# Segment means of h in two whole operations with the sums of h behind them on VectorE, and another order of products in the w3 groups

## The chip, the cores and the metric

The kernel runs on one core of a Trainium2 chip. The core has TensorE (PE, matrix products, with a queue of its own for loading weights, PEld), VectorE (DVE), ScalarE (ACT), GpSimd (POOL) and SyncE (SP, which here only issues DMAs). Each engine works through its instructions in the order of its queue and waits at semaphores for the others. Accumulators lie in eight banks of PSUM, everything else that is worked on in SBUF.

The metric is the time on the device in microseconds, the median of several runs. Before the change it is 1487.03 us (six runs, 1484.1 to 1489.75).

## The reference

A recurrent attention block A and a mixer block B, each between layer norms with conditioning:

```python
x = A_x                                    # 1 x 2048 x 1024
sa, ca, ga, sb, cb, gb = split(silu(c) @ w_mod)
h = layernorm(x) * (1 + ca) + sa
x = x + ga * A(h, mem0, Wq, Wk, Wv, Wo, seg_len=32)
h = layernorm(x) * (1 + cb) + sb
x = x + gb * B(h, w1, w2, w3, w4)

def A(x, mem0, ...):                       # 32 heads of 128, 8 memory rows
    mem = mem0
    for s in range(64):                    # 64 segments of 32 rows
        h = concat([mem, x[segment s]])    # 40 rows
        q, k, v = h @ Wq, h @ Wk, h @ Wv
        o = softmax(mask(q k^T * scale)) v @ Wo
        mem, out_s = o[:8], o[8:]

def B(x, w1, w2, w3, w4):
    h = gelu(layernorm(x) @ w1)
    hs = shifted_quarters(h) @ w2
    x1 = x + hs
    return x1 + gelu(layernorm(x1) @ w3) @ w4     # w3: 1024 x 3584
```

## The kernel before

**Start.** Sixteen row tiles of x are normalized, turned over by TensorE and written as h, transposed, into the tile `hh` (128 partitions, 8 blocks of 128 features, about 2100 columns); lines L436 (VectorE) and L438 (ScalarE) apply the conditioning on the way out of PSUM. Beside each transpose a small product (L427) adds up the 32 rows of every segment into a PSUM bank, `hsum` (named `small_ps` in the profile: 128 partitions, 8 blocks x 64 segments). While later tiles are being normalized, TensorE already runs the projections of the first heads ("wave 0", `proj_main`, L318), whose accumulators are emptied by `evac` (L122 on ScalarE, L127 on VectorE). Three accumulators go round.

**Segment means and the memory.** The memory rows that a segment hands on are first estimated from the segment means. `g_prep` (from L457) makes `hbar`, the means after conditioning, out of `hsum`, the scale `cm` and the shift `sm_`; column 0 is different, since the first segment sees `mem0` (`m0`). Before the change this is one operation per block of features, in turn on ScalarE (L462) and VectorE (L460), then L464 and L465 for column 0. `g_v` multiplies the means by chunks of Wv (L477) and copies the result out (`vbarT`, L478), `g_o` multiplies by chunks of Wo (L491) into a bank that L494 and L495 copy into the memory columns of `hh`. The chunks of 1 MB pass through six buffers `wchunk`, loaded by SP (L473, L487) whenever one is free. One remaining projection of wave 0 is put after each `g_v` or `g_o`. The order of instructions on each engine in this part of the kernel comes from a scheduler that works from the program, its dependencies and estimated times; `keep_order` binds an instruction to its place in the program, and `add_manual_dep` adds a dependency.

**Sums of h.** The main projections of the other heads multiply in two-by-two blocks with seven products instead of eight (Strassen's scheme in Winograd's form). It needs sums of blocks of `hh`: `S1`, `S2`, `S4` and, in place, A11 - A21, for two pairs of column chunks (L519 to L522), and sums `T1` to `T4` of the weights per head (L566 to L569). The products are L623, their results leave through copies (`snap`, L591) and joins (L595). Attention runs between them: scores (L717), exponential (L721, ScalarE), mask (L723, VectorE), products with V (L734, after V was transposed by a DMA, L667), the reciprocals of the sums (L736) and the scaled results `O` (L741 on VectorE, L739 on ScalarE).

**Middle.** The Wo products (L905), the second layer norm, w1 and w2 follow; `Ba` (L1172, L1173) makes x1 and its row sums, `ln_sums` normalizes it, and a DMA transposes it into `z2a` and `z2b`, the two pairs of column chunks of the last stage.

**The w3 and w4 stages** stand in the order of the program on every engine (`manual_schedule`). For each of two pairs, `w3_stage` runs seven groups of 512 columns of w3. A group is again seven products of two halves q, each half four matmuls (L1244). Four banks `bank_b`, two `bank_e` and two `bank_d` hold the results. Products with A11 and B11 start bank_b; ScalarE copies it (`snap`, L1209) as `s1`; products of S2 and T2 are added to the same bank, which is copied again (`s2`); products of S3 and T3 are added, and at last those of A22 and T4. Products of A12 and B21 go to bank_e, products of S1 and T1 to bank_d (copied as `s5`), where those of S4 and B22 are added. `join` adds a bank and a copy on VectorE (L1252), `gelu` follows on ScalarE (L1248). The sums of weights for the next group are L1098, `w3_sums`. The w4 stage (L1295) has the same form over 14 blocks. The next pair starts when the w4 stage of the first ends.

Of the kernel before, what the change touches and what calls it, by code (L numbers as in the profile page):

```python
# [9 lines left out]
BF16 = mybir.dt.bfloat16  # L10
# [9 lines left out]
P = 128  # L20
# [40 lines left out]
def kernel(ctx, tc, A_x, A_mem0, A_Wq, A_Wk, A_Wv, A_Wo, A_seg_len, B_x, B_w1, B_w2, B_w3, B_w4, c, w_mod, out,  # L61
# [105 lines left out]
    def first_pass(late_hook):  # L167
# [288 lines left out]
        def g_prep():  # L456
            gs["hbar"] = sb1.tile([P, KT, NSEG], BF16, name="hbar")  # L457
            for kt in range(KT):
                if kt % 2:
                    nc.vector.tensor_scalar(gs["hbar"][:, kt, :], hsum[:, kt, :], cm[:, kt:kt + 1], sm_[:, kt:kt + 1], ALU.mult, ALU.add)  # L460
                else:
                    nc.scalar.activation(gs["hbar"][:, kt, :], hsum[:, kt, :], ACT.Identity, bias=sm_[:, kt:kt + 1], scale=cm[:, kt:kt + 1])  # L462
            first = sb1.tile([P, KT], F32, name="first")
            nc.vector.tensor_tensor(first[:], hsum[:, :, 0], cm[:], ALU.mult)  # L464
            nc.vector.tensor_tensor(gs["hbar"][:, :, 0], first[:], m0[:], ALU.add)  # L465
            gs["vbarT"] = sb1.tile([P, H, NSEG], BF16, name="vbarT")
# [48 lines left out]
        for p in range(2):  # L515
            c0, c1 = slice(2 * p * CH, (2 * p + 1) * CH), slice((2 * p + 1) * CH, (2 * p + 2) * CH)
            A11, A12, A21, A22 = hh[:, 0:4, c0], hh[:, 4:8, c0], hh[:, 0:4, c1], hh[:, 4:8, c1]
            S1, S2, S4 = (hsp.tile([P, 4, CH], F16, name=f"hs{j}{p}")[:] for j in (1, 2, 4))
            keep_order(nc.vector.tensor_tensor(S1, A21, A22, ALU.add))  # L519
            keep_order(nc.vector.tensor_tensor(S2, S1, A11, ALU.subtract))  # L520
            keep_order(nc.vector.tensor_tensor(S4, A12, S2, ALU.subtract))
            keep_order(nc.vector.tensor_tensor(f16(A21), A11, A21, ALU.subtract))  # L522
            hA.append((A11, A12, S4, A22, S1, S2, f16(A21)))
# [635 lines left out]
        def Ba(t):  # L1159
            def f():  # L1160
# [13 lines left out]
                z = tp.tile([P, D], BF16, name="z")  # L1174
                ln_sums(bsm, z[:], x1b[:], sums)
                zs[t] = z
# [50 lines left out]
        def w3_stage(pair):  # L1227
# [6 lines left out]
            for g in range(7):  # L1234
# [29 lines left out]
                for q in prod("b", S2, T2, False):  # L1264
                    st[q]["s2"] = snap(st2, st[q]["b"])
                for q in range(2):
                    st[q]["d"] = psd.tile([P, 512], F32, name="bank_d")
                for q in prod("d", S1, T1, True):
                    st[q]["s5"] = snap(stA, st[q]["d"])
                for q in prod("b", S3, T3, False):  # L1270
# [815 lines left out]
```

## Time and profile before

| | us |
|---|---|
| median of six runs | 1487.03 (1484.1 to 1489.75) |
| the profiled execution, whole time | 1487.09 |
| its span, first to last instruction | 1485.3 |
| PE busy in the span | 1425.8 (96%) |
| DVE, ACT, POOL busy | 887.4, 684.9, 363.7 |
| PE waiting for hbar (L477) | 4.6, once |
| PE waiting for copies of banks in w3 (L1244) | 8.8, four times |
| one 128x512 f32 sum on DVE (L1252), one copy of a bank on ACT (L1209) | 0.69, 0.58 |
| one 128x1920 sum of h on DVE (L519) | 1.15 |

How to read it: a group line gives the source line, the engine, the operation, what it writes and reads and its shape, and in brackets how long the engine sat idle before it and what ended that idling. Matmuls are pipelined: a 512-wide one is shown as 0.379 us long while the next starts 0.216 us after it. The profile also gives the clock that was granted to TensorE, 0.993 on the mean of this execution.

### The profile page before, as it was taken

What the parts mean: (1) busy time and instruction counts of PE and PEld (TensorE: products, weight loads), DVE (VectorE), ACT (ScalarE), POOL (GpSimd) and SP (SyncE); (2) the same over time, 40 slices, a digit from 0 to 9 for tenths busy, and PEclk for the clock granted to TensorE, in tenths of its full rate; (3) what the DMA queues carried; (4) which work ended last, traced back from release to release, by engine and by line L of the source; (5) the groups of instructions that cost most, each with busy time, mean ns of one, the idle gap of its engine ahead of it and who ended that gap; (6) DMA issues with size and microseconds to landing.
All of it is one profiled execution on the core that took longest, in us unless ns stands there. A gap on an engine that the chain in (4) does not pass through costs nothing. (4 is left out here: it accounts for less than half of the span.)

```text
span 1485.3 us, 24759 instructions
## 1 busy us (share of the span) xinstructions
PE 1425.8 (96%) x9254; PEld 754.8 (51%) x9254; DVE 887.4 (60%) x1946; ACT 684.9 (46%) x1443; POOL 363.7 (24%) x526
## 2 busy tenths in 40 slices
PE   5898999999999999999998999999997999999998
PEld 3565556565555555555554444444443444444443
DVE  5218777777676777667653345344245658666684
ACT  2715666665666665655551021123466661046400
POOL 8402100000000000000001223213023654545525
PEclk9999999999999999999999999999999999999999
DMA  9587967867777777778579999994398774477812
GB/s 321 191 285 157 189 155 184 200 146 173 165 171 177 190 157 179 158 167 183 112 171 315 354 305 369 320 229 156 113 291 244 238 241 149 135 231 250 283 40 78
DMA packets 404149, 303.48 MB, mean 204 GB/s; under 512 B 199082, under 2 KB 356778, under 8 KB 402226
## 3 DMA queue, kind: packets, MB, share of 16 engines
q1 hardware_dynamic: 365904, 242.06, 61.0%
q10 hardware_dynamic: 29330, 30.89, 7.0%
q0 software_dynamic: 8784, 28.85, 6.4%
q8 instruction: 74, 1.21, 0.4%
q14 instruction: 57, 0.47, 0.1%
HBM read 200.56 MB, written 50.63 MB: 169 GB/s over the span
## 5 line engine op out<-in xcount | busy, mean ns | idle before, releaser
L905 PE MATMUL acc<-wstream,OTc 128*128 128x512 bf16 x960 | 209.0, 379 | 5.5 <-DMA OTc<-OTx_d 2.4
L623 PEld LDWEIGHTS <-T 128*128 128x128 f16 x1408 | 130.9, 98 | 119.5 <-issue 2.7
L591 ACT COPY snap<-acc 128x480 f32<-128x480 f32 x264 | 145.9, 563 | 91.2 <-PE acc L623 83.4
L623 PE MATMUL acc<-hh,T 128*128 128x480 bf16 (+1 forms) x704 | 163.8, 367 | 0.0
L623 PE MATMUL acc<-hs,T 128*128 128x480 f16 x704 | 158.3, 367 | 0.7 <-ACT snap L591 0.7
L905 PEld LDWEIGHTS <-OTc 128*128 128x128 bf16 x960 | 93.4, 98 | 117.7 <-issue 3.8
L1244 PEld LDWEIGHTS <-ring 128*128 128x128 f16 (+1 forms) x784 | 77.8, 99 | 107.8 <-issue 17.9
L759 POOL DMA_DIRECT2D OTx_d<-OT x32 | 24.8, 774 | 436.6 <-DMA OT<-O 390.8
L721 ACT ACTIVATE E<-ps_s 99x495 bf16<-99x495 f32 (+2 forms) x160 | 87.1, 545 | 45.9 <-PE ps_s L717 45.4
L623 PE MATMUL acc<-hh,wq 128*128 128x480 bf16 x464 | 103.9, 366 | 0.0
L741 DVE TENSOR_TENSOR O<-ps_o,rin_all 99x384 bf16<-99x384 f32 (+1 forms) x192 | 97.2, 510 | 3.7
L734 PE MATMUL ps_o<-V,E 99*128 99x129 bf16 (+1 forms) x704 | 79.7, 220 | 10.1 <-DMA V<-VT 4.6
L1295 PEld LDWEIGHTS <-hq 128*128 128x128 bf16 (+1 forms) x560 | 54.8, 98 | 66.1
L595 DVE TENSOR_TENSOR KT<-acc,snap 128x480 bf16<-128x480 f32 x116 | 74.9, 655 | 21.2 <-PE acc L623 18.8
L1209 ACT COPY snap<-bank_b 128x512 f32<-128x512 f32 x72 | 40.5, 582 | 100.9 <-PE bank_b L1295 63.2
L1098 DVE TENSOR_TENSOR ring<-ring 128x1024 f16<-128x1024 bf16 (+1 forms) x64 | 80.0, 1270 | 4.4 <-PE bank_b L1295 4.0
L734 PEld LDWEIGHTS <-E 99*128 99x128 bf16 (+1 forms) x704 | 56.3, 98 | 48.0 <-issue 7.5
L1013 ACT ACTIVATE u<-x,ln_nmr,ln_rstd 128x1024 bf16<-128x1024 f32 x16 | 19.7, 1231 | 127.8 <-DVE ln_nmr L1012 125.5
L723 DVE TENSOR_TENSOR E<-E,maskB 99x495 bf16<-99x495 bf16 (+1 forms) x128 | 48.1, 376 | 49.6 <-ACT E L721 47.6
L1295 PE MATMUL bank_b<-ring,hq 128*128 128x512 f16 (+1 forms) x336 | 73.2, 379 | 0.0
L595 DVE TENSOR_TENSOR VT<-acc,snap 128x480 bf16<-128x480 f32 x90 | 58.0, 651 | 24.9 <-PE acc L623 20.8
L1248 ACT ACTIVATE hq<-join 128x512 bf16<-128x512 f32 x84 | 52.8, 630 | 42.6 <-DVE join L1252 42.5
(243 smaller groups left out, 2521.5 us busy)
## 6 DMA issues: line engine op xcount, KB each, us to landing
wstream<-in_A_Wo_dram SPq DMA_DIRECT2D x31, 1024.0 KB, 10.9
OTx_d<-OT POOLq DMA_DIRECT2D x32, 512.0 KB, 7.2
wstream<-in_B_w_dram SPq DMA_DIRECT2D x28, 512.0 KB, 5.7
OTc<-OTx_d SPq DMA_DIRECT2D x14, 1024.0 KB, 8.4
ring<-in_B_w_dram SPq DMA_DIRECT2D x28, 512.0 KB, 6.4
ring<-in_B_w_dram SPq DMA_DIRECT2D x8, 1792.0 KB, 10.9
wq<-in_A_Wq_dram SPq DMA_DIRECT2D x16, 512.0 KB, 5.0
wk<-in_A_Wk_dram SPq DMA_DIRECT2D x16, 512.0 KB, 7.3
```

What stands on the lines that cost most here:

```text
L591: nc.scalar.copy(t[:], st[q][bank][:, 0:CH])
L595: nc.vector.tensor_tensor(view(d, i), chunks(st[q][bank]), chunks(st[q][s_]), ALU.add)
L623: nc.tensor.matmul(acc[:, 0:CH], lhsT=B[:, k, :], rhs=A[:, k, :], start=(j in (1, 2, 5) and k == 0), stop=(k == 3), skip_group_check=True)
L721: nc.scalar.activation(E[:rows, 0:o], ps[:rows, 0:o], ACT.Exp, scale=DH ** -0.5)
L723: nc.vector.tensor_tensor(E[:rows, 0:o], E[:rows, 0:o], mk[:rows, 0:o], ALU.mult)
L734: nc.tensor.matmul(ps[:, i, :], lhsT=state["e", h, t // 5][:k, c:c + P], rhs=V[:k, t, 0:DH + 1], start=True, stop=True)
L741: nc.vector.tensor_tensor(O[:rows, ts[0]:ts[0] + n, :], ps[:rows, 0:n, 0:DH], rin[:, :, None].to_broadcast([rows, n, DH]), ALU.mult)
L905: mm = nc.tensor.matmul(accs[tt][:], lhsT=ot[hl // 4][:, hl % 4, tt * P:(tt + 1) * P], rhs=woc[hl // 4][:, hl % 4, :], start=(h == 0), sto ...
L1098: return nc.vector.tensor_tensor(dst, a, b, op)
L1244: nc.tensor.matmul(acc[:], lhsT=B[:, k, q * P:(q + 1) * P], rhs=A[:, k, :], start=(start and k == 0), stop=(k == 3), skip_group_check=True)
L1248: nc.scalar.activation(hq[a][f][:, g * 2 + q, :], src[:], ACT.Gelu_apprx_tanh)
L1295: nc.tensor.matmul(acc[:], lhsT=L3[:, k, i * P:(i + 1) * P], rhs=R3[:, k, :], start=(start and k == 0), stop=(k == 13), skip_group_check=True)
```

## The change

Three edits. In `g_prep` the means of all blocks are made by two operations on VectorE over the whole tile, with scale and shift broadcast along the segments, and column 0 by a third. The eight sums of h are no longer bound to their place in the program; instead the first of each pair gets a dependency on the last operation of `g_prep`. In `w3_stage` the product of S1 and T1 (bank_d) with its copy stands before the product of S2 and T2 (bank_b) with its copy. In `Ba` an assignment to a Python dictionary moves up by a statement.

```diff
         def g_prep():
             gs["hbar"] = sb1.tile([P, KT, NSEG], BF16, name="hbar")
-            for kt in range(KT):
-                if kt % 2:
-                    nc.vector.tensor_scalar(gs["hbar"][:, kt, :], hsum[:, kt, :], cm[:, kt:kt + 1], sm_[:, kt:kt + 1], ALU.mult, ALU.add)
-                else:
-                    nc.scalar.activation(gs["hbar"][:, kt, :], hsum[:, kt, :], ACT.Identity, bias=sm_[:, kt:kt + 1], scale=cm[:, kt:kt + 1])
-            first = sb1.tile([P, KT], F32, name="first")
-            nc.vector.tensor_tensor(first[:], hsum[:, :, 0], cm[:], ALU.mult)
-            nc.vector.tensor_tensor(gs["hbar"][:, :, 0], first[:], m0[:], ALU.add)
+            hs = sb1.tile([P, KT, NSEG], F32, name="hs")
+            nc.vector.tensor_tensor(hs[:], hsum[:], cm[:, :, None].to_broadcast([P, KT, NSEG]), ALU.mult)
+            nc.vector.tensor_tensor(gs["hbar"][:], hs[:], sm_[:, :, None].to_broadcast([P, KT, NSEG]), ALU.add)
+            gs["done"] = nc.vector.tensor_tensor(gs["hbar"][:, :, 0], hs[:, :, 0], m0[:], ALU.add)
             gs["vbarT"] = sb1.tile([P, H, NSEG], BF16, name="vbarT")
...
-            keep_order(nc.vector.tensor_tensor(S1, A21, A22, ALU.add))
-            keep_order(nc.vector.tensor_tensor(S2, S1, A11, ALU.subtract))
-            keep_order(nc.vector.tensor_tensor(S4, A12, S2, ALU.subtract))
-            keep_order(nc.vector.tensor_tensor(f16(A21), A11, A21, ALU.subtract))
+            s1 = nc.vector.tensor_tensor(S1, A21, A22, ALU.add)
+            tc.add_manual_dep(s1.ins, gs["done"].ins.name, mybir.DependencyInfo(mybir.DependencyClass.Sync, mybir.DependencyReason.DATA), reason="segment means first")
+            nc.vector.tensor_tensor(S2, S1, A11, ALU.subtract)
+            nc.vector.tensor_tensor(S4, A12, S2, ALU.subtract)
+            nc.vector.tensor_tensor(f16(A21), A11, A21, ALU.subtract)
...
-                z = tp.tile([P, D], BF16, name="z")
+                zs[t] = z = tp.tile([P, D], BF16, name="z")
                 ln_sums(bsm, z[:], x1b[:], sums)
-                zs[t] = z
...
                 dve(T4, B21, T2, ALU.subtract)
-                for q in prod("b", S2, T2, False):
-                    st[q]["s2"] = snap(st2, st[q]["b"])
                 for q in range(2):
                     st[q]["d"] = psd.tile([P, 512], F32, name="bank_d")
                 for q in prod("d", S1, T1, True):
                     st[q]["s5"] = snap(stA, st[q]["d"])
+                for q in prod("b", S2, T2, False):
+                    st[q]["s2"] = snap(st2, st[q]["b"])
                 for q in prod("b", S3, T3, False):
                     join(1, 1, q, "b", "s5")
```

## The prediction

> **What bounds the kernel now.** The page first, for which engine carries the span:
>
> ```profile
> span 1485.3 us, 24759 instructions
> PE 1425.8 (96%) x9254; PEld 754.8 (51%) x9254; DVE 887.4 (60%) x1946; ACT 684.9 (46%) x1443; POOL 363.7 (24%) x526
> ```
>
> TensorE is busy for 96%, so only what moves its gaps moves the time. Next the waits of PE (total us, times, longest), where I look for gaps that the edited lines own:
>
> ```profile
> PE bank_b L1244 <- ACT snap L1209: 8.8, 4, 3.2
> PE acc L477 <- DVE hbar L465: 4.6, 1, 4.6
> PE ps_o L734 <- DVE O L741: 3.7, 1, 3.7
> ```
>
> The first is the bank copy in the w3 stage, the second the segment means, the third sits where the sums of h now run. The stages around the last two (length, busy time of each engine, clock, DMA share, GB/s):
>
> ```profile
> 60.00:75.00 15.00, 10.43 (x133) 7.38 (x131) 2.66 (x9) 8.61 (x23) 0.00 (x0) 0.89 0.04 6
> 111.00:130.00 19.00, 14.21 (x126) 9.85 (x125) 15.10 (x27) 9.55 (x28) 9.07 (x12) 0.99 0.88 189
> 130.00:150.00 20.00, 19.87 (x139) 11.41 (x138) 17.81 (x51) 12.25 (x32) 1.60 (x4) 0.92 0.62 132
> 150.00:300.00 150.00, 149.68 (x1104) 88.33 (x1101) 107.72 (x282) 95.02 (x228) 12.88 (x32) 1.00 0.80 178
> ```
>
> PE idles 4.6 us in the first and 4.8 in the second, and loses clock behind each gap (0.89, 0.92); from 150 on it is full, so what is won before stays won. PE's timeline (start, us, what):
>
> ```profile
> 65.23 1.78 PE L318 MATMUL acc<-hh,wk 128*128 128x480 bf16 x8
> 71.59 3.55 PE L477 MATMUL acc<-hbar,wchunk 128*128 128x64 bf16 x64 [4.57 <-DVE hbar L465]
> 74.95 1.84 PE L318 MATMUL acc<-hh,wq 128*128 128x480 bf16 x8
> ...
> 129.44 0.34 PE L734 MATMUL ps_o<-V,E 99*128 99x129 bf16 x3 [3.73 <-DVE O L741]
> 129.62 1.74 PE L623 MATMUL acc<-hh,T 128*128 128x480 f16 x4
> ```
>
> After 4.57 us of idling, 64 matmuls take 3.36 us to the next line; 32 of them take 0.93 further on, so 1.5 us is half clock. After 3.73 us four take 1.74 for 0.97. What ACT and DVE did meanwhile:
>
> ```profile
> 62.48 4.98 ACT L438 ACTIVATE hh<-pt,saT,ca1T 128x160 bf16<-128x160 bf16 x14
> 67.26 0.64 ACT L122 CAST VT<-acc 128x480 bf16<-128x480 f32 x1
> ```
>
> ```profile
> 127.82 0.42 DVE L566 TENSOR_TENSOR T<-wk,wq 128x512 f16<-128x512 bf16 x1 [3.90 <-DMA wk<-in_A_Wk_dram]
> ```
>
> Last, the w3 stage, PE and then ACT:
>
> ```profile
> 1132.67 1.02 PE L1244 MATMUL bank_b<-zs,ring 128*128 128x512 f16 x4 [1.66 <-ACT snap L1209]
> ...
> 1140.32 3.41 PE L1244 MATMUL bank_b<-zs,ring 128*128 128x512 f16 x8 [2.45 <-ACT snap L1209]
> ...
> 1164.29 1.89 PE L1244 MATMUL bank_d<-zs,ring 128*128 128x512 f16 x8
> ...
> 1311.02 3.40 PE L1244 MATMUL bank_b<-zs,ring 128*128 128x512 f16 x8 [3.25 <-ACT snap L1209]
> ```
>
> ```profile
> 1165.41 0.59 ACT L1209 COPY snap<-bank_d 128x512 f32<-128x512 f32 x1 [0.26 <-PE bank_d L1244]
> ...
> 1310.38 1.07 ACT L1209 COPY snap<-bank_b 128x512 f32<-128x512 f32 x2 [29.56 <-DMA xb<-x1b_d]
> ```
>
> Only the first group of each pair has gaps; twelve of fourteen are gapless.
>
> **The change part by part**
>
> *Segment means.* Removed: four ACT and four DVE operations in turn (0.40 and 0.34 us) and two small ones. The chain was slow because its ACT half stood behind L438 and three L122 evacuations: it began at 62.17 and ended at 71.46. Added, all on DVE, free at 62.40: a product out of PSUM, a sum, and the first column. A 128x512 f32 operation of two tensors takes 0.69 (L1252), the column 0.20 (L465): done near 64.0. PE ends its L318 at 66.85, so the means no longer hold it. What is late next is the accumulator: the first Wv product takes the one that ACT evacuates at 67.26 to about 67.85. PE restarts at 67.9, after 1.05 us of idling instead of 4.57: 3.7 us. Gaps of 1.66 and 1.43 us in the w3 stage are followed by full spacing (four matmuls in 1.02), those of 2.03 and more by half, so I take full clock: 1.5 us more. Together **-5.2**. Bounds: -3.7 (half clock after all) to -5.4. The weight chunks issued after each freed slot move with PE: the one freed first landed 7.3 to 8.6 us after its issue and is needed 12.7 us after.
>
> *Sums of h.* Seven of the eight 128x1920 sums (1.07 us apart) leave the stretch 111 to 122 and run behind the means. In the built order five stand ahead of the first vbarT copy, two between copies. From 64.0 five end at 69.4, the copy at 69.8; PE wants that accumulator back for the third Wv product at about 71.4, after two Wv products and an L318. Later copies have over 1 us too. Who reads vbarT comes 20 us later. Cost 0, covered by those matmuls; with the sums held until the last h is written (67.3) it would be 2.3 us of PE. The in-place sum of the first pair waits for a product that runs at 62, the other stays near 111.
>
> At 111 DVE now finishes its T sums at about 115 instead of 122.2, so the masks of E follow ACT's exponentials (118.35 on) at once, and the T sum that waits for wk (127.82, a DMA issued behind two transposes on SP) stands behind the first two O's in the queue instead of ahead of them. On old times: the first outs products wait for the transpose of V issued at 113.64, which lands 7.2 us on, 120.84 (1.45 us of PE idle, for 0.89 at 122.69 before). Walking the new PE order from there with 0.2 us per 480-wide matmul, PE meets the queue behind the T sum near 129.9 and loses about 0.5, 0.2, 0.3 and 0.5 us in short waits, and reaches the L328 products of the second group at 133.6 instead of 137.18: **-3.6**. Bounds: -1.9 (a half-clock stretch after the 1.45) to -6.1 (0.89 + 3.73 idle and 1.5 of clock all gone).
>
> *w3 order.* Old order: bank_b, bank_e, bank_b (S2,T2), bank_d (S1,T1), bank_b (S3,T3). Each bank_b product waits for ACT's copy of what it adds to. With bank_d ahead, the S2 product has more cover and the S3 product has none but the other half of S2. ACT's queue changes alike: copies of bank_d ahead of the second of bank_b.
> First group of pair 0: bank_d fills the 1.66 us gap, but the end is set by ACT, whose two gelus wait until 1138.57 for a join that waits for the last transpose of z. Then come two copies more ahead of the one PE waits for, 0.47 apart: S3 starts at 1141.28 instead of 1140.32, **+1.0** (0.9 to 1.1), half clock behind it as before.
> First group of pair 1: ACT is held until 1310.38 by the output DMAs. Before, S2 ran at 1311.02 at half clock (3.25 for 1.73), then bank_d, and S3 at 1315.98. Now bank_d runs in the gap (its T1 is ready by 1307.4), S2 at 1311.02 after 1.7 us of idling at full clock, copies at 1312.92, 1313.39 and 1313.87, S3 at 1314.5: **-1.5**. Bounds -1.5 to +0.2 (half clock).
> Gapless groups: no row shows a product on the bank just copied. Nearest is bank_d at 1164.29: its copy begins 1.12 us after the product and ends at 1165.99; PE goes on 0.055 after a copy (1310.965 to 1311.02), thus 1.76 after the start, where two products take 1.727. So 0.03 per group, **+0.4** in twelve; bounds 0 and 0.2 x 12 = 2.4 (a copy that begins late by an idle stretch of ACT, 0.26).
>
> [...] The rows: gaps of 2.45 and 3.25 us each cost a stretch of 3.3 us at half speed, 1.4 and 1.7 did not. [...] I stay with the rows.
>
> *The rest.* `zs[t]` in Ba is assigned one statement earlier: no instruction, 0. No DMA is added or removed, and the queues of SP and POOL keep their order. Behind PE's order from about 140 to the w3 stage nothing differs.
>
> **Sum.** -5.2 - 3.6 + 1.0 - 1.5 + 0.4 = -8.9 against the profiled execution: span 1485.3, 1487.09 in all, which is 0.06 above the median 1487.03. Result **1478**.
>
> **Rivals**
> - *DMA holds the second gap anyway.* If V's transpose or wk comes later than read here, PE waits in place of DVE, and only the means pay: 1487.1 - 5.2 - 0.1 = 1482. For: the 3.90 us of wk. Against: its T sum now stands behind work PE needs. 0.17.
> - *Sums ahead of the copies stall the Wv products*: +2.3, 1480.5. For: five in one queue. Against: the first four read h written before 60, and only the fifth reads the last chunk. 0.10.
> - *Slower: the S3 product waits out both copies.* If PE resumes only when the second copy is done, 1.12 + 0.86 + 0.585 + 0.055 = 2.62 for 1.73, 0.9 per group, 12.6 in fourteen, +3.3 with the other terms: 1490.5. It decides from 0.66 us per group on. For: the margin is under zero. Against: each half waits for its own copy. 0.05.
> - *The change does not do what it says*: PE would be held at 67 by the accumulator for as long as by the means. Its evacuation at 67.26 excludes more than 1.1 us of that.
>
> **Numbers.** Likeliest case 0.65, the three rivals 0.32, the rest 0.03. Its own range is 1474 (all upper gains) to 1481.5; with the first two rivals and the medians' scatter 1473.5 to 1483.5, leaving out the slow one and tails. About 0.2% (3 us) is what a measurement can tell: faster means below 1484.1, which holds the likeliest case and nearly all of the first two rivals, 0.90; same 0.05; slower 0.05.
>
> **What would show it.** L477 starting 1 us after L318 at full spacing; no 3.7 us wait on O; S3 of pair 0 about 1 us later after its gap and of pair 1 sooner; gaps of some 30 ns before S3 in the other groups. Wrong if those gaps exceed 0.2 us, if PE idles 2 us or more before the third Wv product, or if a half-clock stretch follows the short gaps.

## The result, and the profile after

The changed kernel takes 1480.25 us (median of 20 runs, 1478.37 to 1483.86) against 1486.65 us for the kernel before (46 runs): a ratio of 0.9957, 95% interval 0.9947 to 0.9967, 6.4 us faster. The profiled execution has a span of 1477.9 us, 1479.68 in all; both are 7.4 below those of before. The head of its page:

```profile
span 1477.9 us, 24760 instructions
...
PE 1422.9 (96%) x9254; PEld 752.4 (51%) x9254; DVE 884.6 (60%) x1943; ACT 684.0 (46%) x1439; POOL 360.7 (24%) x526
```

**Segment means.** TensorE's timeline of the changed kernel around them (start, us, what, and in brackets the idle time before and what ended it):

```profile
65.73 1.78 PE L318 MATMUL acc<-hh,wk 128*128 128x480 bf16 x8
68.49 2.03 PE L473 MATMUL acc<-hbar,wchunk 128*128 128x64 bf16 x64 [0.98 <-ACT VT L122]
70.35 1.78 PE L318 MATMUL acc<-hh,wq 128*128 128x480 bf16 x8
```

and VectorE's:

```profile
62.80 0.68 DVE L459 TENSOR_TENSOR hs<-small_ps,cm 128x512 f32<-128x512 f32 x1
63.52 0.69 DVE L460 TENSOR_TENSOR hbar<-hs,sm 128x512 bf16<-128x512 f32 x1
64.25 0.19 DVE L461 TENSOR_TENSOR hbar<-hs,m 128x8 bf16<-128x8 f32 x1
64.58 1.16 DVE L515 TENSOR_TENSOR hs<-hh 128x1920 f16<-128x1920 bf16 x1
...
70.05 0.42 DVE L474 CAST vbarT<-acc 128x256 bf16<-128x256 f32 x1
```

The means are done at 64.44 us (64.25 and 0.19). TensorE waits 0.98 us, for the accumulator that ScalarE empties and not for them, and its 64 matmuls take 1.86 us to the next line instead of 3.36. The first vbarT copy ends at 70.47; the third product of means and Wv, which needs that accumulator, starts at 71.97, without a wait.

**The stretch where the sums of h were.** First the stages (length, busy time of PE, PEld, DVE, ACT, POOL with instruction counts, clock, DMA share, GB/s), then the waits of 0.7 us and more that TensorE still has in the stretch, with the second group's wv products (L328):

```profile
60.00:75.00 15.00, 14.02 (x199) 9.14 (x198) 11.11 (x16) 8.30 (x21) 0.00 (x0) 1.00 0.28 90
111.00:130.00 19.00, 16.38 (x126) 9.57 (x124) 10.20 (x28) 9.80 (x24) 3.80 (x7) 1.00 0.95 207
130.00:150.00 20.00, 18.74 (x146) 11.01 (x144) 16.21 (x48) 14.12 (x36) 1.86 (x5) 1.00 0.86 176
```

```profile
116.22 0.33 PE L731 MATMUL ps_o<-V,E 104*128 104x129 bf16 x3 [1.32 <-DMA V<-VT]
...
125.97 0.34 PE L731 MATMUL ps_o<-V,E 99*128 99x129 bf16 x3 [0.72 <-DVE E L720]
...
129.08 1.53 PE L328 MATMUL acc<-hh,wv 128*128 128x199 bf16 x16 [0.16 <-DVE VT L592]
...
135.29 0.40 PE L731 MATMUL ps_o<-V,E 99*128 99x129 bf16 x4 [1.05 <-DVE E L720]
```

The same wv products before:

```profile
137.18 1.54 PE L328 MATMUL acc<-hh,wv 128*128 128x199 bf16 x16
```

The 3.73 us wait for O is gone, the wait for the transpose of V has come (1.32), and the second group's wv products start at 129.08. Counted from the wk product ahead of the means (65.73, before 65.23) that is 63.35 us instead of 71.95: 8.6 us won. The last line is new: a wait of 1.05 us. ScalarE shows why:

```profile
131.44 2.01 ACT L679 ACTIVATE wstream<-wstream 128x2048 bf16<-128x2048 bf16 x1
...
133.35 0.67 ACT L718 ACTIVATE E<-ps_s 99x495 bf16<-99x495 f32 x1
```

The exponential that this E needs stands behind a square of the weight guard (L679), which adds up the squares of a part of w3. When it is done, at 134.02, VectorE has an O and a product of a row ahead of the mask, which starts at 134.82. At a mark far behind, the product that waits for a transpose of V at 625 us, the lead is smaller. After and before:

```profile
624.99 0.33 PE L731 MATMUL ps_o<-V,E 104*128 104x129 bf16 x3 [0.90 <-DMA V<-VT]
```

```profile
631.76 0.33 PE L734 MATMUL ps_o<-V,E 104*128 104x129 bf16 x3 [0.90 <-DMA V<-VT]
```

Counted in the same way it is 7.3 us (559.26 against 566.53): 1.3 of the 8.6 were given back.

**The w3 stage.** TensorE in the first group of pair 0 and of pair 1, then what ScalarE and VectorE did in pair 0:

```profile
1117.76 1.89 PE L1240 MATMUL bank_b<-z2a,ring 128*128 128x512 bf16 x8 [1.86 <-POOL ln_ve L1149]
...
1127.18 1.50 PE L1240 MATMUL bank_b<-zs,ring 128*128 128x512 f16 x4 [1.43 <-ACT snap L1205]
1133.45 3.57 PE L1240 MATMUL bank_b<-zs,ring 128*128 128x512 f16 x8 [4.77 <-ACT snap L1205]
1136.82 2.39 PE L1240 MATMUL bank_d<-zs,ring 128*128 128x512 f16 x8
1139.05 3.62 PE L1240 MATMUL bank_b<-z2a,ring 128*128 128x512 bf16 x16
...
1304.93 1.89 PE L1240 MATMUL bank_b<-zs,ring 128*128 128x512 f16 x8 [1.52 <-ACT snap L1205]
1308.36 1.89 PE L1240 MATMUL bank_b<-zs,ring 128*128 128x512 f16 x8 [1.55 <-ACT snap L1205]
```

```profile
1130.72 1.23 ACT L1244 ACTIVATE hq<-join 128x512 bf16<-128x512 f32 x2 [3.59 <-DVE join L1248]
1131.86 1.05 ACT L1205 COPY snap<-bank_d 128x512 f32<-128x512 f32 x2
1132.80 1.08 ACT L1205 COPY snap<-bank_b 128x512 f32<-128x512 f32 x2
```

```profile
1130.00 1.29 DVE L1248 TENSOR_TENSOR join<-bank_e,snap 128x512 f32<-128x512 f32 x2 [11.99 <-DMA z2b<-z]
```

The first and the seventh product of pair 0 before:

```profile
1125.71 2.95 PE L1244 MATMUL bank_b<-z2a,ring 128*128 128x512 bf16 x8 [2.03 <-POOL ln_ve L1152]
...
1145.30 3.62 PE L1244 MATMUL bank_b<-z2a,ring 128*128 128x512 bf16 x16
```

In pair 0 the product with S3 waits 4.77 us and then runs at half clock (eight matmuls in 3.57 us, elsewhere in 1.89; the granted clock is 0.50 from 1133.5 to 1136.5). What it waits for is a chain: its copy stands behind the copies of bank_d, these behind the gelus, these behind joins, and the first join waits for the last transposes of z. From the first product of the group to the seventh (A22 by T4, the first eight of the sixteen at 1139.05) it takes 21.29 us; before 19.59. S3 starts 15.69 us after the first product, before 14.61. In pair 1 there are two short waits at full clock (eight matmuls in 1.89 behind each), 13.75 us to the seventh product; before it was 15.28, with one wait of 3.25 us and half clock behind it (eight in 3.40, granted clock 0.50). The other twelve groups repeat every 12.11 us, before 12.08.

### The profile page after: what moved, and what is told of

It reads as the page before. It is cut to its first block, busy times and chain, and to the rows that moved or that the text cites. A ratio compares the mean times of both kernels' runs of the same rounds, so it can differ in the third digit from the quotient of the medians.

```text
span 1477.9 us, 24760 instructions
## 1 busy us (share of the span) xinstructions
PE 1422.9 (96%) x9254; PEld 752.4 (51%) x9254; DVE 884.6 (60%) x1943; ACT 684.0 (46%) x1439; POOL 360.7 (24%) x526
## 5 line engine op out<-in xcount | busy, mean ns | idle before, releaser
L620 PEld LDWEIGHTS <-T 128*128 128x128 f16 x1408 | 130.6, 97 | 119.5 <-issue 2.0
L620 PE MATMUL acc<-hh,T 128*128 128x480 bf16 (+1 forms) x704 | 163.1, 366 | 0.3 <-DVE VT L592 0.3
L620 PE MATMUL acc<-hs,T 128*128 128x480 f16 x704 | 157.1, 366 | 0.7 <-ACT snap L588 0.6
L620 PE MATMUL acc<-hh,wq 128*128 128x480 bf16 x464 | 103.9, 366 | 0.0
L592 DVE TENSOR_TENSOR VT<-acc,snap 128x480 bf16<-128x480 f32 x90 | 58.1, 652 | 24.8 <-PE acc L620 20.4
```

The costliest lines, as they stand in the source:

```text
L592: nc.vector.tensor_tensor(view(d, i), chunks(st[q][bank]), chunks(st[q][s_]), ALU.add)
L620: nc.tensor.matmul(acc[:, 0:CH], lhsT=B[:, k, :], rhs=A[:, k, :], start=(j in (1, 2, 5) and k == 0), stop=(k == 3), skip_group_check=True)
```

## The experiments

All were run beside the kernel before, whose medians were 1485.5 to 1487.3 us. Executions reach the wk product ahead of the means 64.97 to 66.38 us after their start, so positions in this table are counted from that product, in us; below it is called the reference product. "To w3" is where the first w3 product starts, "w3 on" the time from there to the end of the span, the next two the first group of each pair from its first to its seventh product.

| kernel | 2nd group's wv products | to w3 | w3 on | pair 0 | pair 1 | median (runs) | ratio to before (95%) |
|---|---|---|---|---|---|---|---|
| before | 71.95 | 1060.48 | 359.59 | 19.59 | 15.28 | 1486.65 (46) | |
| after | 63.35 | 1052.03 | 360.14 | 21.29 | 13.75 | 1480.25 (20) | 0.9957 (0.9947, 0.9967) |
| a_means | 66.76 | 1054.64 | 356.79 | 18.12 | 13.77 | 1480.22 (8) | 0.9962 (0.9948, 0.9976) |
| b_front | 63.27 | 1051.85 | 357.07 | 18.29 | 13.77 | 1477.59 (12) | 0.9949 (0.9933, 0.9965) |
| c_w3 | 72.12 | 1059.50 | 359.71 | 20.84 | 13.75 | 1487.93 (12) | 1.0007 (0.9996, 1.0018) |
| d_p1 | 63.10 | 1051.73 | 356.83 | 18.09 | 13.81 | 1476.56 (6) | 0.9939 (0.9922, 0.9956) |
| v1_gelu | 63.41 | 1053.70 | 354.23 | 16.21 | 12.27 | 1476.13 (4) | 0.9931 (0.9914, 0.9947) |
| m_pool | 62.96 | 1050.47 | 356.66 | 15.70 | 13.75 | 1475.01 (4) | 0.9921 (0.9904, 0.9937) |
| o_pool | 63.08 | 1053.19 | 356.55 | 15.46 | 13.77 | 1482.96 (10) | 0.9969 (0.9953, 0.9986) |
| g_guard | 63.08 | 1058.16 | 361.69 | 22.10 | 13.75 | 1487.95 (10) | 1.0009 (0.9999, 1.0018) |
| f_wk | 68.52 | 1056.54 | 359.23 | 20.43 | 13.75 | 1483.06 (1) | |
| v2_new0 | 63.21 | 1052.81 | 361.08 | 23.17 | 12.28 | 1481.91 (5) | 0.9961 (0.9947, 0.9975) |
| v2_guard | 63.11 | 1058.08 | 362.25 | 25.25 | 12.27 | 1487.09 (11) | 1.0001 (0.9991, 1.0011) |
| m_late1 | 63.39 | 1056.39 | 355.39 | 15.70 | 12.27 | 1475.06 (5) | 0.9928 (0.9914, 0.9943) |

"To w3" scatters: after, v1_gelu, m_pool and m_late1 issue the same instructions up to there and lie between 1050.47 and 1056.39. A single profile thus places the w3 stage only to some 6 us, while a group within it is read to a few hundredths. Its length can still differ from execution to execution: pair 0's first group, with the same w3 instructions in after, c_w3, f_wk and g_guard, takes 20.43 to 22.10 us. The scatter comes in behind the 625 us mark: there the eight kernels with the front of the changed one (after, b_front, d_p1, v1_gelu, m_pool, o_pool, v2_new0, m_late1) lie between 558.85 and 559.94, a_means at 561.42 and before at 566.53. The ratios are each taken beside their own runs of the kernel before. Medians of different kernels are not: where two are compared below, differences of 2 us, the spread of the medians of the kernel before, show nothing by themselves.

### The three parts, one by one

**a_means**: the changed kernel with the sums of h kept in place and the old order in w3 (the edit of b_front, below, besides this one).

```diff
-            s1 = nc.vector.tensor_tensor(S1, A21, A22, ALU.add)
-            tc.add_manual_dep(s1.ins, gs["done"].ins.name, ...)
+            keep_order(nc.vector.tensor_tensor(S1, A21, A22, ALU.add))
...
```

> Only the segment means are new; the sums of h stay where the kernel before has them and the w3 groups keep the old order. Theory (the parts add up): TensorE starts the first Wv product about 1 us after the last wk product instead of 4.6, at full clock, and the second wq product stands 5.1 us earlier, as in the changed kernel; the sums still stand in the stretch from 111 to 137 us, so nothing more is won there: 5.2 us faster than before, about 1481.5 us, with the first V-and-E product of the second head pair's stretch and the 16 wv products behind it only some 5 us earlier than before. Rival (the transfers hold the stretch from 111 to 137): what is won at 72 us is waited away there, and less than 3 us of it is left at the end.

TensorE in the stretch:

```profile
124.12 0.51 PE L730 MATMUL ps_o<-V,E 99*128 99x129 bf16 x3 [3.74 <-DVE O L737]
...
131.83 1.54 PE L328 MATMUL acc<-hh,wv 128*128 128x199 bf16 x16
```

The 3.74 us wait for O is back and everything behind it stands 5.2 us earlier than before (66.76 against 71.95). The means' gain passes the stretch whole, and 5.1 us of it stand at the 625 us mark. The rival falls. By the ratio 5.7 us are won (3.6 to 7.7). So the means alone are as fast as the whole change, 1480.22 against 1480.25 us: what the sums of h win, the order of the products loses again.

**b_front**: the changed kernel with the old order in w3.

```diff
-                for q in range(2):
-                    st[q]["d"] = psd.tile([P, 512], F32, name="bank_d")
-                for q in prod("d", S1, T1, True):
-                    st[q]["s5"] = snap(stA, st[q]["d"])
                 for q in prod("b", S2, T2, False):
                     st[q]["s2"] = snap(st2, st[q]["b"])
+                for q in range(2):
+                    st[q]["d"] = psd.tile([P, 512], F32, name="bank_d")
+                for q in prod("d", S1, T1, True):
+                    st[q]["s5"] = snap(stA, st[q]["d"])
```

> The changed kernel with the old order of the products in all w3 groups: means and sums of h new, nothing else. Theory: means 5.2 and stretch 3.6 us, less about 1.3 us that the changed kernel's trace shows given back at 135 us: 7.5 us faster than before; in the first group of pair 0 the product with S3 starts about 1 us earlier than in the changed kernel and the half clock ends sooner (1.7 us in all), in the first group of pair 1 it starts 1.5 us later, and the other twelve groups are 0.03 us shorter: some 0.6 us faster than the changed kernel in sum, 1479 to 1480 us. Rival (the new order of the products is what shortens w3): slower than the changed kernel by 1 us or more.

Against a_means the sums of h bring 3.5 us at the wv products (63.27 against 66.76), 2.2 at the 625 us mark (559.22 against 561.42), 2.6 in the medians. Against the changed kernel the old order is 2.7 us faster in the median and 3.07 in "w3 on", several times the 0.6 expected. By the ratios it is only 1.2 us, with intervals that overlap; two of the twelve runs took 1484.81 and 1486.87 us, the others at most 1480.79. TensorE in both first groups:

```profile
1129.31 3.62 PE L1240 MATMUL bank_d<-zs,ring 128*128 128x512 f16 x8
1132.92 2.03 PE L1240 MATMUL bank_b<-zs,ring 128*128 128x512 f16 x8
...
1302.23 1.89 PE L1240 MATMUL bank_b<-zs,ring 128*128 128x512 f16 x8 [3.25 <-ACT snap L1205]
```

In pair 0 the half clock falls on the product of bank_d, which only fills the time until the copy of s2 is there; S3 follows at once at nearly full speed. In pair 1 the same wait of 3.25 us as before is followed by eight matmuls in 1.89, not in 3.40. So neither first group of the kernel before shows what the order costs: both were longer in its one profiled execution because half clock fell on products that others waited for. S3 of pair 0 starts at the same distance from the first product in both (14.61 before, 14.69 here); it is the half clock on S3 itself (3.41 us for its eight matmuls before, 2.03 here) that makes the difference of 1.3 us.

**c_w3**: the kernel before with the new order in w3 alone (the edit of b_front backwards).

> The kernel before with the new order in the w3 groups alone. Theory: the first group of pair 0 loses 1.0 us at the product with S3 and up to 0.7 more by a longer half clock, the first group of pair 1 wins 1.5, the other twelve lose 0.03 each: between 0.1 us faster and 0.6 slower than before, no difference that these rounds can show for sure. Rival (each group saves a wait for the copies of the kept bank): 0.1 us or more in each of 14 groups, over 1.4 us faster; rival (the copies of s2, which now come last before S3, are waited for in each group): 0.66 us or more in each group, 9 us slower.

1.1 us slower in the median, the interval from 0.6 faster to 2.7 slower: no difference shown, though the interval just reaches the 2.7 us of b_front; both rivals with gains or losses in every group are out. Pair 0 takes 20.84 (19.59 before), pair 1 13.75 (15.28), about as in the changed kernel.

**d_p1**: the changed kernel with the new order in the first group of pair 1 alone.

```diff
+                for part in (d_part, s2_part) if pair == 1 and g == 0 else (s2_part, d_part):
+                    part()
```

> The changed kernel with the new order of the products in the first group of pair 1 alone, the old one in the other thirteen groups. Theory: the 1.7 us of pair 0's first group and the 0.4 us of the twelve gapless groups come back and the 1.5 us of pair 1's first group stay: about 2.1 us faster than the changed kernel, 8.5 us faster than before, and the faster of the two against the kernel with the old order everywhere by 1.5 us. Rival (the two first groups cannot be told apart, since what pair 1 wins at S3 is lost in the same group behind it): as fast as the old order everywhere.

It is 3.7 us faster than the changed kernel by the medians (2.1 expected) and 3.3 in "w3 on"; 3.2 are pair 0, 18.09 against 21.29, the rest the gapless groups. But pair 1 takes 13.81 us with the new order and 13.77 with the old one (b_front), and "w3 on" is 356.83 against 357.07. The rival's outcome came, but not its reason: S3 starts 10.36 us after the group's first product here and 10.31 with the old order, so nothing was won at S3 that could be lost again. The new order brings nothing in pair 1 when the old one is not hit by half clock.

### What holds the product with S3 in pair 0

**v1_gelu**: the gelus of bank_e behind the copies.

```diff
                 for q in prod("e", A12, B21, True):
-                    join(0, 0, q, "e", "s1")
+                    t = stm.tile([P, 512], F32, name="join")
+                    nc.vector.tensor_tensor(t[:], st[q]["e"][:], st[q]["s1"][:], ALU.add)
+                    held.append(t)
...
                 for q in prod("b", S2, T2, False):
                     st[q]["s2"] = snap(st2, st[q]["b"])
+                for q in range(2):
+                    gelu(0, 0, q, held[q])
```

> The changed kernel with the two gelus of bank_e issued behind the copies s5 and s2 in each w3 group, nothing left out. Theory: in the first group of pair 0 S3 starts 15.7 us after the group's first product because its copy s2 stands on ScalarE behind gelus whose joins wait for the last transposes of z. With the gelus behind, only the memory of s2 still waits for them, until about 12.3 us: S3 at some 12.9 us and the second group about 3 us earlier, 4.5 if the half clock goes too; in the first group of pair 1 S3 starts 1.1 us earlier: 4 to 5.5 us faster than the changed kernel, 1475 to 1476 us. Rival (the copy of s2 itself is what is late, or the half clock): S3 at 15 us or later and no gain over 1.5 us.

```profile
1132.83 1.89 PE L1240 MATMUL bank_b<-zs,ring 128*128 128x512 f16 x8 [2.30 <-ACT snap L1205]
```

S3 starts 12.76 us after the group's first product (12.9 expected, 15.69 in the changed kernel), at full clock; the seventh product comes 5.1 us sooner, and in pair 1 the second of the two waits is gone (12.27). 4.1 us faster than the changed kernel by the medians, 5.9 in "w3 on". Theory held.

**m_pool**: the same instructions as the changed kernel, other addresses.

```diff
-        hq_p = ...
-        ring_pools[1] = ...
-        stA = ...
         st2 = ...
+        stA = ...
         stm = ...
+        hq_p = ...
+        ring_pools[1] = ...
         rsq = ...
```

> The changed kernel with the buffers of the copies and joins of the w3 groups allocated ahead of hq and of the second weight ring, so that they no longer lie where z and x1b lay; same instructions. Theory: the joins of bank_e (idle 12 us on VectorE before the first, released by the transposes of z) go as soon as the copies s1 are there, the gelus behind them, and S3 of pair 0's first group starts 12.0 to 12.6 us after the group's first product instead of 15.7; the second group stands 3.3 us earlier, up to 5 if the half clock goes too; pair 1 as before: 3.3 to 5 us faster than the changed kernel. Rival: the load of the third group's weights now waits for the transposes instead, and TensorE waits for it at the third group; then less than 1 us is won.

TensorE and VectorE:

```profile
1128.09 1.89 PE L1240 MATMUL bank_b<-zs,ring 128*128 128x512 f16 x8 [1.81 <-ACT snap L1205]
```

```profile
1122.78 0.69 DVE L1248 TENSOR_TENSOR join<-bank_e,snap 128x512 f32<-128x512 f32 x1 [6.70 <-ACT snap L1205]
```

The first join is released by the copy s1, not by the transposes. S3 starts 12.25 us after the first product (12.0 to 12.6 expected), the seventh product 5.6 us sooner than in the changed kernel. So the wait for the transposes was one for memory that is used twice, not for data. 5.2 us faster than the changed kernel by the medians. Not all of the 5.6 us stays: "w3 on" is only 3.5 shorter, with a new wait of 1.46 us in the fifth group (below) and 0.7 us that are not placed. The rival, a wait for the third group's weights, did not come.

**o_pool**: these buffers with the old order (the edits of m_pool and b_front together).

> As m_pool (buffers of copies and joins ahead of hq and the second ring), but with the old order of the products in all w3 groups. Theory: what the new order costs in pair 0's first group is a matter of the copies waiting for the transposes alone. Without that wait the old order has the copies s2 made while S1 by T1 runs, S3 starts some 12.0 us after the group's first product (12.25 in m_pool) and the second group some 15.4 (15.7): the orders are within 0.5 us of each other there, pair 1's first group is 1.5 us longer than in m_pool, the other twelve 0.03 shorter each: 0.5 to 1.2 us slower than m_pool. Rival (the new order loses in pair 0 in any case, since s2 is copied last): 1 us or more faster than m_pool.

S3 starts 12.01 us after the first product and without a wait, the seventh product at 15.46, as worked out (12.0 and 15.4). So the 3 us that the new order loses in pair 0 exist only while the copies stand behind the joins that wait for that memory. "W3 on" equals m_pool's, 356.55 against 356.66. The median of 1482.96 doesn't fit: ten runs lie between 1476.9 and 1488.1, evenly spread, where m_pool's four lie within 1.6 us. The profiled one was the fastest. What makes the others slower is open. So with the old order the buffers' new place brings nothing that the times show: b_front, with the old place, has a median of 1477.59.

### What is left of the stretch at 111 to 137 us

**g_guard**: the first squares of the weight guard later.

```diff
-            for i in range(28):
+            units += [nop, nop, nop, nop, load(0), square(0), load(1), square(1)]
+            for i in range(2, 28):
                 units += [load(i), nop, nop, square(i)]
```

> The changed kernel with the first two squares of the weight guard moved about six ScalarE instructions later, nothing left out. Theory: the first V-and-E product behind the second group's wv products waits 1.05 us (69.6 us after the last wk product before the means) because its E is exponentiated behind the first square of 2.0 us; with the square later that wait is under 0.3 us, the change's gain in the stretch is 0.8 to 1.0 us larger, and the kernel that much faster than the changed one. Rival (VectorE's row products in front of the mask hold it): the wait stays over 0.7 us and the time does not move.

The wait of 1.05 us did go (0.60 is left, for an O). But the load of the first square moved too, and ScalarE's queue held an exponential behind it:

```profile
147.32 1.91 ACT L679 ACTIVATE wstream<-wstream 128x2048 bf16<-128x2048 bf16 x1 [8.11 <-DMA wstream<-in_B_w_dram]
...
149.23 0.32 ACT L719 ACTIVATE E<-ps_s 99x198 bf16<-99x198 f32 x1
```

TensorE waited 5.51 us for that E and ran at half speed behind it (eight matmuls of 199 columns in 1.49 us, sixteen in 1.53 at 128.13). At the next full wq product (L620) it stood 7.2 us behind the changed kernel (89.19 against 82.03 us after the reference product), at the 625 us mark 7.5. 1487.95 us, as slow as before: a square that waited for its load lost what the change had won. Neither the theory nor the rival foresaw this.

**f_wk**: the weights of the third head pair on GpSimd's queue.

```diff
-                nc.sync.dma_start(t[nm][:], wslice(W2, hp * 256, 256))
+                (nc.gpsimd if hp == 2 else nc.sync).dma_start(t[nm][:], wslice(W2, hp * 256, 256))
```

> The changed kernel with the q, k and v weights of the third head pair loaded on GpSimd's queue instead of behind the transposes of V on SP's. Theory (the rest of the second gap is this load's landing): VectorE's first T sum of wk starts up to 3.9 us earlier than in the changed kernel, the waits of 0.72, 0.27 and 0.16 us go, and the 16 wv products of the second group start about 1.1 us earlier, 62.2 us after the last wk product before the means instead of 63.35; the 1.32 us wait for V's transpose stays. Rival (the transposes and this load share the engines that move them): V lands later by as much, the 1.32 us grow, and the wv products start no earlier.

VectorE and TensorE:

```profile
123.06 0.43 DVE L563 TENSOR_TENSOR T<-wk,wq 128x512 f16<-128x512 bf16 x1 [4.47 <-DMA wk<-in_A_Wk_dram]
```

```profile
124.68 0.51 PE L731 MATMUL ps_o<-V,E 99*128 99x129 bf16 x3 [4.20 <-DVE O L738]
```

wk was issued 50.1 us after the reference product (at 115.52) instead of 51.6 (117.37), and the sum that it releases starts at the same place, 57.6 us after it in both. The queue that the load stands in didn't set when it landed (in the slice of the page from 111 to 148 us the DMA engines are busy for 8 tenths here, 9 in the changed kernel), so the theory falls; V's wait stayed at 1.33, so the rival's half of V paying for it falls too. On top, the scheduler put the T sums that wait for wk ahead of an O that TensorE needs. This is the order of the kernel before, and its wait came back, 4.20 us: the second group's wv products start at 68.52 instead of 63.35. The one run took 1483.06 us.

### Combinations

**v2_new0**: new order and held gelus in the first group of each pair alone, with the buffers of copies and joins first.

```diff
+        stA, st2, stm, rsq, ring_pools[1], hq_p = ...        # in this order
...
+                    if g:
+                        gelu(0, 0, q, t)
+                    else:
+                        held.append(t)
...
+                for part in (d_part, s2_part) if g == 0 else (s2_part, d_part):
+                    part()
+                for q, t in enumerate(held):
+                    gelu(0, 0, q, t)
```

> The changed kernel with three things together: the new order of the products in the first group of each pair alone, there with the gelus of bank_e behind the copies s5 and s2, and the buffers of copies and joins ahead of the second ring and hq (ring ahead of hq). Theory: in pair 0 S3 starts 10.9 to 11.2 us after the group's first product (12.25 in m_pool) and the second group at about 14.4 us (15.7); in pair 1 the second of the two 1.5 us waits goes; twelve groups of 12.08 instead of 12.11 us: about 3 us faster than m_pool, 1472 us, 14.5 to 15.5 us faster than before. Rival (the half clock sets in as the waits are spread): S3 as early as that, but the second group over 16 us after the first product, and no faster than m_pool by over 1 us.

1481.91 us. S3 of pair 0 waits 9.40 us, because the scheduler moved the last row's shift of z (L1154) behind the copies of bank_d, and GpSimd's part of that row behind a product whose load had not come. ScalarE, then GpSimd:

```profile
1134.31 1.24 ACT L1154 ACTIVATE z<-x1b,ln_nmr,ln_rstd 128x1024 bf16<-128x1024 f32 x1 [8.12 <-POOL ln_nmr L1153]
```

```profile
1128.34 1.26 POOL L1217 TENSOR_TENSOR xb<-xb,gb_b 128x512 f32<-128x512 f32 x1 [6.47 <-DMA xb<-x1b_d]
...
1131.97 0.18 POOL L1149 TENSOR_SCALAR ln_ve<-ln_sq 128x1 f32<-128x1 f32 x1
```

Neither the theory nor its rival had this; the early S3 was not reached, so it doesn't speak on the half clock.

**v2_guard**: the same with the first square four units later, its load in place.

```diff
-            for i in range(28):
+            units += [load(0), nop, nop, nop, nop, nop, nop, square(0)]
+            for i in range(1, 28):
                 units += [load(i), nop, nop, square(i)]
```

> As v2_new0, with the first square of the weight guard four units later and its load where it was (in g_guard the load was moved too, and the square waited for it until 147 us with an E behind it). Theory: the wait of 1.05 us at the first V-and-E product behind the second group's wv products falls to the 0.60 us that g_guard's trace shows there or less, nothing waits for the square later, and the kernel is 0.4 to 1.0 us faster than v2_new0. Rival (ScalarE is where the stretch ends, whichever instruction stands first): the wait comes back at the next E and the time does not move.

1487.09 us, 5.2 slower than v2_new0. The wait fell to 0.61 us, and up to the wait for V at the 625 us mark TensorE was 2.1 us ahead (557.85 against 559.94 after the reference). Against the changed kernel that is 1.4 us ahead, so 8.7 of the 8.8 us won at the wv products were kept up to there. Then a wait of 2.08 us for a K came at 568, where VectorE has six products of a row (L267, 0.48 us each in the changed kernel) ahead of the join that makes it, and by the first w3 product it was 5.3 us behind, which is within the scatter of that mark. S3 of pair 0 waits 10.22 us, 0.8 more than in v2_new0. The squares behind the first had moved too; what makes the kernel 5.2 us slower is open.

**m_late1**: m_pool with the held gelus in the first group of pair 1 alone.

```diff
+                    if pair == 1 and g == 0:
+                        held.append(t)
+                    else:
+                        gelu(0, 0, q, t)
```

> m_pool with the two gelus of bank_e behind the copies s5 and s2 in the first group of pair 1 alone; the order of the instructions elsewhere is that of m_pool. (In v2_new0 the last row's shift of z was moved behind the copies of d, and waited for a GpSimd product that itself waited for a load; here it stands where m_pool has it.) Theory: the second of the two waits of 1.5 us in that group goes as in v1_gelu, and nothing else moves: 1.5 us faster than m_pool, some 1473.5 us, 13 to 14 us faster than before. Rival (the medians of these kernels scatter between chips by more than that, as the kernel with the old order and these buffers showed with 1476.9 to 1488.1 us): the profile shows the wait gone and the median lies between 1476 and 1483 us all the same.

Pair 1 takes 12.27 us in place of 13.75, and from its seventh product to the end 166.0 us as in m_pool: the 1.5 us are in the profile. The medians don't show them: 1475.06 us, ratio 0.9928 against 0.9921 for m_pool, each beside its own runs of the kernel before, with intervals that overlap. The profiled execution is the slowest of its five (1479.19 us), late already at "to w3"; the other four lie between 1474.4 and 1475.1. The rival's median of 1476 to 1483 us did not come either. m_pool and m_late1 are the fastest kernels of the study, 10 to 12 us below the kernel before and about 5 below the changed one.

## Why the prediction was right, and where its terms were not

The forecast was 1478.0 us in a range of 1473.5 to 1483.5, and faster; measured 1480.25. The direction and the first two terms held; the third did not. The time alone shows little of this: the range is 10 us wide, the means without the other two edits came out at the same 1480.2, and two rivals, at 1480.5 and 1482, lie nearer to the measured time than the likeliest case. It is the traces that exclude them. Its terms:

- *Segment means, -5.2*: right in size and in cause. 5.1 us between L318 and the next wq product, full clock behind the short wait of 0.98 us (64 matmuls in 1.86), and what is late next is the accumulator, as written (the first Wv product starts 2.76 us after the reference product, 2.67 forecast). a_means carries 5.2 us through the stretch and 5.7 to the end by its ratio.
- *Sums of h, cost 0*: right. No product of means and Wv waits, the first copy has 1.5 us to spare.
- *Sums of h, -3.6 in the stretch*: right where it was read, 3.5 us between b_front and a_means at the wv products, with the forecast waits at V (1.32 for 1.45) and behind it. But 2.2 to 2.6 us reach the end. The step stopped at the L328 products and took it that nothing behind them could be late; the exponential behind the guard's square was. g_guard and v2_guard moved the square, the wait went from 1.05 to 0.6, and v2_guard kept 8.7 of its 8.8 us up to the 625 us mark. That the square alone costs the 1.3 us is not shown, since other squares moved with it.
- *w3 order, -0.1 in all*: this is the term that was mis-sized. Against the old order behind the same front it is +1.2 us by the ratios, +2.7 by the medians and +3.07 in the profiles. Pair 0: S3 was said to start 1.0 us later, which it does (15.69 for 14.61), with 0.6 us more of half clock behind it than before (5.60 us from S3 to the seventh product for 4.98); but this is against a profile in which the old order had half clock on S3. The old order in a_means, b_front and d_p1 takes 18.1 to 18.3 us to the seventh product, the new one in the changed kernel, c_w3, f_wk and g_guard 20.4 to 22.1. Pair 1: the -1.5 appeared between the two profiles and is no effect of the order (13.75 against 13.77). Twelve groups at 0.03: right, 12.11 against 12.08.
- The step that failed is thus the clock: "I stay with the rows", which took it that gaps of 2.0 us and more cost a stretch of half clock and 1.7 does not. The same trace of the kernel before has rows against it, of which this is one:

```profile
800.48 7.08 PE L905 MATMUL acc<-wstream,OTc 128*128 128x512 bf16 x32 [2.44 <-DMA OTc<-OTx_d]
```

These 32 matmuls behind a gap of 2.44 us take as long as the next 32, which have none (7.07); behind gaps of 2.12 and 2.38 us at 721.58 and 816.85 the granted clock is 1.00 too. And the sign that would show it wrong, half clock behind a short gap, came: behind 1.43 us four matmuls of S2 take 1.50 us in the changed kernel and 1.87 in c_w3, for 1.02 before. What decides whether a gap costs clock is not shown.
- *The range*: the bounds of the terms add up to -12.1 and -1.9 us, 1475 and 1485, where the text has 1474 and 1481.5. On the slow side the stated range is thus narrower than its own terms.

The sum of what was measured, 5.7 to 6.6 us for the means, 2.6 for the sums, +2.7 for the order, is -5.6 to -6.5, the measured -6.4. With 6.6 this agreement shows nothing, since the three terms are differences along one chain of medians and add up by construction; the count by the two profiles is independent of it. There 8.45 us are won up to the first w3 product and 0.55 lost behind it, and the reference product itself comes 0.50 later: 7.4 of the forecast 8.9.

The rivals: wk's landing does hold its T sum (4.47 us in f_wk, 3.92 in the changed kernel), but that sum no longer stands ahead of what TensorE needs, as the prediction said against that rival; put back there, it costs 5.2 us. That DMA leaves only the means to pay did not come: 2.2 us of the sums are there at the 625 us mark. Sums that stall the Wv products, and an S3 product that waits out both copies in each group, did not come either.

## What to carry to other kernels

In a queue that runs in order, look at what stands behind the instruction that waits: three of the largest losses here (4.77, 5.51 and 9.40 us of TensorE) were copies or exponentials that had their inputs and stood behind something waiting for a load or for memory in second use. When the first operation of a stage waits for a transfer that has nothing to do with its data, look at the addresses: with the new order, putting the small buffers elsewhere took 5.6 us off the first group, more than any order of the products alone; with the old order it took 2.8 us off the group (15.46 for 18.29) and nothing that shows off the time. Don't price a half-clock stretch from one profile; compare two executions that have the same gap first.

## What the runs showed of the hardware that was not expected

**The same gap cost clock in one run and not in another.** Ahead of the first w3 product, m_pool, v1_gelu and m_late1, one line each:

```profile
1115.84 1.89 PE L1240 MATMUL bank_b<-z2a,ring 128*128 128x512 bf16 x8 [1.96 <-POOL ln_ve L1149]
```

```profile
1120.07 3.12 PE L1240 MATMUL bank_b<-z2a,ring 128*128 128x512 bf16 x8 [1.97 <-POOL ln_ve L1149]
```

```profile
1122.11 3.55 PE L1240 MATMUL bank_b<-z2a,ring 128*128 128x512 bf16 x8 [1.99 <-POOL ln_ve L1149]
```

Eight matmuls take 1.89, 3.12 and 3.55 us after gaps of 1.96, 1.97 and 1.99. After 3.25 us they took 3.40 before and 1.89 in b_front, and 1.89 after 3.24 us in o_pool. It was half speed behind each of the following nine gaps. Eight matmuls took 3.57 us after 4.39 (c_w3), 4.77 (the changed kernel) and 10.22 (v2_guard), and 3.36 after 9.40 (v2_new0). Four matmuls of 480 columns took 1.74, 1.80 and 1.81 after 3.73 (before), 3.74 (a_means) and 4.20 (f_wk), elsewhere 0.97. The other two are the 4.57 us ahead of the means before (64 matmuls in 3.36 us, 1.86 in the changed kernel) and the 5.51 in g_guard. In b_front, after a gap of 3.35 us in pair 0, four matmuls ran at full spacing (1.02), and half speed (1.87 for four) set in 2.5 us after the end of that gap, behind a further one of 1.43. What decides it is not shown.

**Three sums on VectorE took 6.03 us while GpSimd worked and 2.01 while it was idle.** In the fifth group of m_pool, VectorE and GpSimd:

```profile
1168.85 6.03 DVE L1095 TENSOR_TENSOR ring<-ring 128x1024 f16<-128x1024 bf16 x3
```

```profile
1169.17 1.28 POOL L1217 TENSOR_TENSOR xb<-xb,gb_b 128x512 f32<-128x512 f32 x1
1170.53 1.61 POOL L1218 TENSOR_TENSOR x<-xb,x 128x512 f32<-128x512 f32 x1
...
1173.04 1.28 POOL L1217 TENSOR_TENSOR xb<-xb,gb_b 128x512 f32<-128x512 f32 x1
```

In the changed kernel three such sums run while GpSimd is idle (from 1175.98 to 1178.68):

```profile
1176.26 2.01 DVE L1095 TENSOR_TENSOR ring<-ring 128x1024 f16<-128x1024 bf16 x3
```

Three sums of weights that take 0.67 us each there take 6.03 while GpSimd works on its addends; the join of bank_e behind them comes late (at 1174.80), and so the 1.46 us wait in this group. m_late1 waits 1.00 us for the same product in its fourth group and 0.69 in its fifth. That GpSimd's work is what lengthens the sums, and that TensorE's wait follows from it, is read from these rows and was not tried.
